# The attention's low halves of two batches: a VectorE subtraction becomes a TensorE pass and a ScalarE copy, in a new order

## The chip, the cores and the metric

The kernel runs on one core of one Trainium2 chip. The metric is device microseconds of one execution, from launch to end; a comparison takes the median of several. PE is TensorE, PEld its weight loads, DVE is VectorE, ACT is ScalarE, POOL is GpSimd, and SP is SyncE, which issues all the DMAs of this kernel.

## The reference

Three stages follow one another, all in float32: attention over pooled keys and values, a gated MLP with a convolution of three taps along the sequence, and a second gated MLP that mixes along the sequence.

```python
# q, k, v: (8, 8, 576, 64); keys and values are means over 8 neighbours
k_p = k.reshape(B, H, 72, 8, D).mean(axis=3)
v_p = v.reshape(B, H, 72, 8, D).mean(axis=3)
attn = softmax(q @ k_p.T / 8)             # 1e-9 added to the sum
x = (attn @ v_p).transpose(0, 2, 1, 3).reshape(8, 576, 512)
...
h = np.maximum(x @ w_in, 0.0)             # 512 -> 1024
conv_out = sum(conv_w[k] * shift(h, k - 1) for k in range(3))
x = h * sigmoid(conv_out) @ w_out
...
h = gelu(x @ w_in2)                       # 512 -> 1024, halves u and v
v_s = einsum('ts,bsd->btd', w_sg, normalize(v) * g_ln) + b_sg
out = x + (u * v_s) @ w_out2
```

## The kernel before

**Split numbers.** TensorE multiplies operands of the type fp32r. So that the result comes out as accurate as float32, an operand is held as two such numbers, a high half (the value rounded to fp32r) and a low half (the value less the high half, rounded again), and a product is a sum of three passes: high by high, low by high, high by low. Each operand therefore costs a rounding copy, mostly on ACT, and a subtraction, on DVE or POOL.

**Stages.** Batches are worked on one after another, 576 rows each. For a batch `t_k` and `t_v` pool keys and values, `t_kfin` and `t_vfin` lay them out as `KBT` and as `Vh`, `Vl`, `VR`; `t_qtr` transposes the queries (batches 0 and 1 by PE, the others by DVE); `t_s` forms the scores and the softmax; `t_e` transposes its result into `eTh` and `eTl`, again by PE for batches 0 and 1 (`B_DMA = 2`) and by way of DRAM and DVE (`xb`) for the others. `t_a` then multiplies by the values: for each pair of heads p and each half of the rows it sums four passes of 128 x 288 into a bank of PSUM and leaves the result, divided by 8 (the keys' and values' pool), as the high half `xT[0]` (tile `xh`) and the low half `xT[1]` (tile `xl`). The in-projection `t_i` reads `xh` and `xl`, 384 columns at a time and twelve passes for each of eight column blocks, and does the convolution and the gate on ACT and DVE; `t_o` is the out-projection. The second MLP follows from about 540 us on.

**What t_a does in batches 0 to 7.** Four passes on PE (L523, through the helper at L106), a copy of the bank times 1/8 by ACT into `xh` (L531), and one DVE instruction (L533) that takes the bank times 1/8 less `xh` into `xl`. The bank comes from `a_bank`, which has three buffers that scores, transposes and `t_a` share; it is free again when the DVE instruction has read it.

**Weights.** The weights arrive as 64-bit numbers. `to_f32` turns each 128 x 512 block into float32 with three DVE instructions (L146, L149, L152); ACT then copies the high half (L209) and POOL subtracts (L134). These 16 blocks (`wi0` to `wi7`, `w0` to `w7`) are needed in the first 120 us.

**Order.** Every engine runs its instructions in the order in which they are written, and that order is given by hand in the string `ORDER`: some 3,600 words such as `a2.0` (one more step of task `a`, part 2, batch 0), each of which runs one step of a generator up to its next `yield`. A waiting instruction holds up all that stands behind it on its engine. SP issues the DMAs in the same order.

Of the kernel before, what the change touches and what calls it, by code (L numbers as in the profile page):

```python
# [26 lines left out]
def pooled_attention_gated_mlps(  # L27
# [37 lines left out]
    TT = [(t * 128, min(128, S - t * 128)) for t in range((S + 127) // 128)]  # L65
    NM = S // 128
# [22 lines left out]
    def a_bank():  # L89
        return psum1.tile([128, 512], F32, tag="a", bufs=3, name="psa")  # L90
# [24 lines left out]
    ident = const.tile([128, 128], F32, name="ident")
    small = const.tile([128, 6], F32, name="small")
    mask, mhalf = small[0:96, 0:4], small[:, 4:6]
    coef = const.tile([128, 32], F32, name="coef")

    in1_ctx = ExitStack()  # L120
    in1 = in1_ctx.enter_context(tc.tile_pool(name="in1", bufs=1))
    att_ctx = ExitStack()
    att1 = att_ctx.enter_context(tc.tile_pool(name="att1", bufs=1, side="right"))
    att2 = att_ctx.enter_context(tc.tile_pool(name="att2", bufs=2, side="right"))
    KBT = att1.tile([128, NP_, 2 * SP], F32, name="KBT")
    Vh = att1.tile([128, NP_, 128], F32R, name="Vh")
    Vl = att1.tile([128, NP_, 128], F32R, name="Vl")
    VR = att1.tile([96, NP_, 128], F32R, name="VR")
    eTh = att1.tile([128, NP_ + 2, S], F32R, name="eTh")
    eTl = att1.tile([128, NP_, S], F32R, name="eTl")  # L130
# [5 lines left out]
    def to_f32(raw, t, tmp=None):  # L136

        w = raw.rearrange("p (n t) -> p t n", t=2)
        lo, up = w[:, 0, :], w[:, 1, :]
        ti = t.bitcast(U32)
        mi = ti if tmp is None else tmp.bitcast(U32)
        nc.vector.tensor_scalar(out=mi, in0=up, scalar1=3, scalar2=0x3FFFFFF8,  # L146
                                op0=ALU.logical_shift_left, op1=ALU.bitwise_and)
        yield
        nc.vector.scalar_tensor_tensor(out=mi, in0=up, scalar=0xC0000000, in1=mi,  # L149
                                       op0=ALU.bitwise_and, op1=ALU.bitwise_or)  # L150
        yield
        nc.vector.scalar_tensor_tensor(out=ti, in0=lo, scalar=29, in1=mi,  # L152
                                       op0=ALU.logical_shift_right, op1=ALU.bitwise_or)
        yield
# [22 lines left out]
    def t_coef(*_):  # L177
        n = 3 * NF
        cf = work.tile([128, 512], F32, tag="y", name="cf")
        raw = att2.tile([128, 1024], U32, tag="raw", name="craw")  # L180
        nc.sync.dma_start(out=raw[0:n, 0:256], in_=conv_w.rearrange("k (m p) -> (k m) p", p=256))
        nc.sync.dma_start(out=cf[n:n + NU, 0:128], in_=g_ln.rearrange("(m p) -> m p", p=128))
        yield
        yield from to_f32(raw[0:n, 0:256], cf[0:n, 0:128])
        ps = a_bank()
        n += NU
        nc.tensor.transpose(ps[:, 0:n], cf[0:n, 0:128], ident[0:n, 0:n])
        yield
        nc.scalar.copy(out=coef[:, 0:n], in_=ps[:, 0:n])

    def cw(kk, m):
        return coef[:, kk * NF + m:kk * NF + m + 1]

    def gl(m):
        return coef[:, 3 * NF + m:3 * NF + m + 1]


    def weight(pool_, tag, src, eng, bank_, done):
        raw = pool_.tile([128, 1024], U32, tag=tag, name=f"{tag}raw")
        dst = raw  # L200
        if len(src.shape) == 3:
            dst = raw.rearrange("p (a b) -> p a b", a=src.shape[1])
        nc.sync.dma_start(out=dst, in_=src)
        yield
        t = work.tile([128, 512], F32, tag="y", name="t")
        yield from to_f32(raw, t, bank_() if bank_ else None)
        hl = pool_.tile([128, 2, 512], F32R, tag=tag, name=f"{tag}hl")
        done(hl)
        nc.scalar.copy(out=hl[:, 0, :], in_=t)  # L209
        yield  # L210
        subtract(hl[:, 1, :], t, hl[:, 0, :], eng)
# [25 lines left out]
    def staged(name, n, where=None):  # L237

        if where is not None:
            p_, tag, size = where  # L240
            early[name] = [p_.tile([128, size], F32, tag=tag, name=name), 0]
        z, at = early[name]
        early[name][1] += 512 * n
        return z[:, at:at + 512 * n].rearrange("p (a s) -> p a s", a=n)
# [125 lines left out]
    qbs = {}  # L370
    qTs = {}

    def t_q(_, b):
        qb = att1.tile([128, len(TT) * DM], F32, tag="qb", name="qb")[:, 0:NP_ * S].rearrange("p (a s) -> p a s", a=NP_)
        for c in range(4):
            for pr in range(NP_):
                nc.sync.dma_start(
                    out=qb[32 * c:32 * c + 32, pr, :],
                    in_=q[b, 2 * pr + c // 2, :, 32 * (c % 2):32 * (c % 2) + 32].rearrange("(g i) d -> i g d", i=32),
                )  # L380
        qbs[b] = qb

    def t_qtr(t, b):
        t0, n = TT[t]
        if b < 2:
            if t == 0:
                if b == 0:
                    z = staged("q0", 5, (in1, "xl", XW * KC))
                else:
                    z = att1.tile([128, len(TT) * DM], F32, tag="qb", name="qb").rearrange("p (t d) -> p t d", d=DM)  # L390
                qbs[b] = z
            nc.sync.dma_start(out=qbs[b][0:n, t, :].rearrange("p (h d) -> p h d", h=H),
                              in_=q[b, :, t0:t0 + n, :].rearrange("h s d -> s h d"))
            yield
            ps = a_bank()
            for p in range(NP_):
                nc.tensor.transpose(ps[:, 128 * p:128 * p + n], qbs[b][0:n, t, 128 * p:128 * p + 128],
                                    ident[0:n, 0:n])
            yield
            qT = att2.tile([128, NP_, 128], F32, tag="qT", name="qT")  # L400
            nc.scalar.copy(out=qT[:, :, 0:n], in_=ps.rearrange("p (a s) -> p a s", a=NP_)[:, :, 0:n])  # L401
        else:
            qT = att2.tile([128, NP_, 128], F32, tag="qT", name="qT")
            nc.vector.transpose(out=qT[:, :, 0:n], in_=qbs[b][:, :, t0:t0 + n])
        qTs[b, t] = qT
# [104 lines left out]
    xT = {}  # L510
# [7 lines left out]
    def t_a(p, b):  # L518
        x0 = (b % 2) * (S + 2) + 1
        for hf in range(2):  # L520
            ps = a_bank()[:, 0:HS]
            T = slice(HS * hf, HS * hf + HS)
            mm_sum(ps, [  # L523
                (Vh[:, p, :], eTh[:, p, T]),
                (Vh[:, p, :], eTl[:, p, T]),
                (Vl[:, p, :], eTh[:, p, T]),
                (VR[:, p, :], eTh[0:96, NP_ + p // 2, T]),
            ])
            yield
            X = slice(x0 + HS * hf, x0 + HS * hf + HS)  # L530
            nc.scalar.activation(out=xT[0][:, p, X], in_=ps, func=AF.Copy, scale=1.0 / POOL)  # L531
            yield
            nc.vector.scalar_tensor_tensor(  # L533
                out=xT[1][:, p, X], in0=ps, scalar=1.0 / POOL, in1=xT[0][:, p, X].bitcast(F32),
                op0=ALU.mult, op1=ALU.subtract)
            yield
# [73 lines left out]
    w2 = {}  # L610
# [153 lines left out]
    def passes(ps, pairs, first, last):  # L764
        n = len(pairs)
        for i, (a, b_) in enumerate(pairs):
            nc.tensor.matmul(out=ps, lhsT=a, rhs=b_, start=first and i == 0, stop=last and i == n - 1,  # L767
                             skip_group_check=True)
# [191 lines left out]
    g2 = {}  # L960
# [126 lines left out]

    for key in ORDER.split():
        step(key)
# [30 lines left out]
```

## Time and profile before

| | before |
|---|---|
| time, median of 3 runs | 953.7 us (951.04, 953.7, 954.91) |
| the profiled execution, its own time | 952.67 us |
| its span, first to last instruction | 950.9 us |
| PE busy | 918.5 us (97%) |
| PE weight loads busy | 838.4 us (88%) |
| DVE busy | 759.8 us (80%) |
| ACT busy | 527.6 us (55%) |
| POOL busy | 553.5 us (58%) |
| mean granted TensorE clock | 0.993 of 2.4 GHz |

The span leaves out 1.77 us of the execution's own time. An engine's busy time is the time in which at least one of its instructions runs; PE's matmuls overlap, so that one takes longer from start to end than the next needs to start after it. In the profile an idle time is put down to the instruction that the engine waited for, its releaser.

### The profile page before, as it was taken

How to read it: one execution, taken by the hardware profiler on the slowest of the kernel's cores; microseconds unless marked ns; L12 is line 12 of the kernel's file. 1: busy time of each engine (PE TensorE's matmuls, PEld its weight loads, DVE VectorE, ACT ScalarE, POOL GpSimd, SP SyncE). 2: the span in 40 equal slices, each digit the busy share in tenths (PEclk: the TensorE clock that was granted, in tenths of full speed). 3: DMA queues.
4: the chain of work that ended last, by engine and by line, in shares of the span. 5: the costliest groups of instructions: out<-in, count | busy, mean ns of one | idle time of the engine just before them, and what ended most of it. 6: DMA issues, size and time to landing. Idle time of an engine off the chain costs nothing.

```text
span 950.9 us, 15815 instructions
## 1 busy us (share of the span) xinstructions
PE 918.5 (97%) x5396; PEld 838.4 (88%) x5396; DVE 759.8 (80%) x1399; ACT 527.6 (55%) x1108; POOL 553.5 (58%) x630
## 2 busy tenths in 40 slices
PE   5899999999999999999999999999999899999998
PEld 4787789988899899998998899999999898999886
DVE  5889988879879687787687878888787977878574
ACT  3666576766667576666655757655656432323211
POOL 3696788785868676557245375643553665555331
PEclk9899999999999999999999999999999999999999
DMA  9986293744635644424380475466537755565734
GB/s 230 251 197 149 62 186 114 178 133 139 153 119 139 142 119 100 129 59 117 99 170 34 94 144 141 151 184 200 146 111 230 246 176 190 158 192 173 231 115 142
DMA packets 185900, 143.61 MB, mean 151 GB/s; under 512 B 106048, under 2 KB 140124, under 8 KB 185820
## 3 DMA queue, kind: packets, MB, share of 16 engines
q1 hardware_dynamic: 185820, 142.61, 56.4%
q8 instruction: 42, 0.69, 0.3%
q14 instruction: 38, 0.31, 0.1%
HBM read 94.20 MB, written 48.37 MB: 150 GB/s over the span
## 4 chain that ended last, share of the span: by engine, by line
PE 77%; DVE 9%; DMA 6%; POOL 2%; ACT 2%; issue 2%; SPq 1%; DVEq 0%; POOLq 0%; ACTq 0%
PE psi L106 19%; PE pso L767 12%; PE psa L767 12%; PE pso L99 6%; PE pso L101 6%; PE pso L100 6%; PE psi L101 3%; PE psi L99 3%; PE psi L100 3%; PE psa L106 3%; PE psa L419 3%; DMA st<-in_v_dram 2%; DMA res<-x2s 1%; DMA wi1raw<-in_moe_w_in_dram 1%; DVE psi L571 1%
## 5 line engine op out<-in xcount | busy, mean ns | idle before, releaser
L134 POOL TENSOR_TENSOR hg<-g,hg 128x384 fp32r<-128x384 f32 x96 | 97.5, 1023 | 64.0 <-ACT hg L580 60.3
L1001 POOL TENSOR_TENSOR u<-u,tmp 128x288 f32<-128x288 f32 x64 | 61.8, 986 | 56.0 <-DVE tmp L997 39.8
L573 ACT ACTIVATE psi<-psi 128x384 f32<-128x384 f32 x96 | 46.1, 480 | 68.2 <-DVE psi L571 68.1
L570 DVE SCALAR_TENSOR_TENSOR psi<-h,coef,psi 128x384 f32<-128x384 f32 x96 | 58.9, 614 | 26.4 <-ACT psi L568 25.4
L134 POOL TENSOR_TENSOR eTl<-xb,eTh 128x512 fp32r<-128x512 f32 (+1 forms) x30 | 45.3, 1510 | 50.2 <-ACT eTh L503 50.1
L708 POOL TENSOR_TENSOR xb<-xb 128x768 f32<-128x768 f32 x24 | 45.9, 1912 | 48.2 <-DVE xc L134 30.2
L558 ACT ACTIVATE h<-psi 128x386 f32<-128x386 f32 (+1 forms) x96 | 47.3, 493 | 43.6 <-PE psi L106 43.3
L577 DVE SCALAR_TENSOR_TENSOR g<-psi,h 128x384 f32<-128x384 f32 x96 | 52.4, 546 | 20.0 <-ACT psi L573 18.1
L617 ACT CAST sc<-vf 128x512 fp32r<-128x512 f32 x48 | 28.8, 618 | 63.1 <-POOL vf L948 27.8
L571 DVE SCALAR_TENSOR_TENSOR psi<-h,coef,psi 128x384 f32<-128x384 f32 x96 | 59.8, 623 | 3.4
L419 PE MATMUL psa<-KBT,qT 128*128 128x144 f32 (+1 forms) x320 | 54.0, 299 | 5.2 <-ACT qT L401 1.8
L568 ACT ACTIVATE psi<-h,coef 128x384 f32<-128x384 f32 x96 | 56.2, 586 | 3.1
L419 PEld LDWEIGHTS psa<-KBT,qT 128*128 128x128 f32 (+1 forms) x320 | 45.2, 184 | 12.8 <-ACT qT L401 2.4
L580 ACT CAST hg<-g 128x384 fp32r<-128x384 f32 x96 | 47.7, 507 | 10.1 <-DVE g L577 10.0
L767 PE MATMUL pso<-wc,xc 128*128 128x256 f32 x378 | 51.1, 283 | 1.3 <-ACT tmp L790 0.9
L767 PE MATMUL psa<-wc,xc 128*128 128x256 f32 x378 | 50.7, 282 | 0.8 <-ACT tmp L790 0.5
L767 PEld LDWEIGHTS pso<-wc,xc 128*128 128x128 f32 x378 | 48.5, 189 | 2.5 <-ACT tmp L790 1.3
L1016 ACT CAST g<-u 128x256 fp32r<-128x256 f32 x64 | 22.3, 402 | 50.4 <-POOL u L1001 43.2
L767 PEld LDWEIGHTS psa<-wc,xc 128*128 128x128 f32 x378 | 48.6, 189 | 1.4 <-ACT tmp L790 0.7
L767 PE MATMUL psa<-xc,wc 128*128 128x384 f32 x252 | 48.2, 338 | 0.3 <-ACT tmp L834 0.3
L767 PE MATMUL pso<-xc,wc 128*128 128x384 f32 x252 | 48.3, 338 | 0.0
L457 POOL TENSOR_TENSOR en<-e,rs 128x512 f32<-128x512 f32 (+1 forms) x30 | 32.7, 1091 | 23.2 <-ACT h L558 8.5
(397 smaller groups left out, 3106.0 us busy)
## 6 DMA issues: line engine op xcount, KB each, us to landing
xb<-eds SPq DMA_DIRECT2D x24, 384.0 KB, 3.1
x2s<-ob SPq DMA_DIRECT2D x36, 256.0 KB, 2.8
us<-ub SPq DMA_DIRECT2D x24, 384.0 KB, 3.3
vs<-vg SPq DMA_DIRECT2D x18, 512.0 KB, 3.7
u<-us SPq DMA_DIRECT2D x16, 576.0 KB, 5.0
vf<-vs SPq DMA_DIRECT2D x16, 512.0 KB, 3.8
out_dram<-ob SPq DMA_DIRECT2D x32, 256.0 KB, 2.9
xb<-x2s SPq DMA_DIRECT2D x40, 192.0 KB, 4.3
```

Source lines behind the costliest of these rows:

```text
L99: nc.tensor.matmul(out=out_, lhsT=ah, rhs=bh, start=first, stop=False)
L100: nc.tensor.matmul(out=out_, lhsT=al, rhs=bh, start=False, stop=False)
L101: nc.tensor.matmul(out=out_, lhsT=ah, rhs=bl, start=False, stop=last)
L106: nc.tensor.matmul(out=out_, lhsT=a, rhs=b_, start=(i == 0), stop=(i == n - 1))
L134: eng.tensor_tensor(out=out, in0=in0, in1=hi.bitcast(F32), op=ALU.subtract)
L419: nc.tensor.matmul(out=ps[0:n, 2 * SP * x:2 * SP * x + 2 * SP], lhsT=qT[:, p, 0:n], rhs=KBT[:, p, :], start=True, stop=True)
L568: nc.scalar.activation(out=y, in_=tap(1), func=AF.Copy, scale=cw(1, f))
L570: nc.vector.scalar_tensor_tensor(out=y, in0=tap(0), scalar=cw(0, f), in1=y, op0=ALU.mult, op1=ALU.add)
L571: nc.vector.scalar_tensor_tensor(out=y, in0=tap(2), scalar=cw(2, f), in1=y, op0=ALU.mult, op1=ALU.add)
L577: nc.vector.scalar_tensor_tensor(out=go, in0=y, scalar=1.0, in1=tap(1), op0=ALU.add, op1=ALU.mult)
L767: nc.tensor.matmul(out=ps, lhsT=a, rhs=b_, start=first and i == 0, stop=last and i == n - 1, skip_group_check=True)
L1001: pool.tensor_tensor(out=z, in0=z, in1=o, op=ALU.mult)
```

## The change

In `t_a`, for batches 0 and 1 alone, the DVE instruction goes. In its place PE adds to the same bank a fifth pass, the high half `xh` times a new constant `minus` (minus 8 times the identity, 128 x 128), and ACT copies what is then in the bank, times 1/8, to `xl`. The five passes go through `passes`, which starts the bank's sum at the first pass and ends it at the fifth; the ACT copy to `xh` reads the sum in between. `minus` is made once by an ACT instruction in `t_coef`. Batches 2 to 7 are as before.

The tile `qb` holds 2,304 numbers for each partition in place of 2,560: of batch 1's five pieces of queries the last, of 64 rows, now lies in the tile `xb` (named `qe` there). `ORDER` is written anew from end to end; it has 16 words more, two for each of `a0.0` to `a3.1`.

```diff
-ORDER = '''z k0.0 k1.0 k2.0 z z p0.0 c p1.0 p2.0 v0.0 v1.0 p3.0 p4.0 v2.0 i0 i1 z z k0.1 p0.0 k1.0 ...'''
+ORDER = '''z k0.0 k1.0 k2.0 z z p0.0 c p1.0 p2.0 v0.0 v1.0 p3.0 p4.0 v2.0 i0 i1 z z k0.1 v2.1 p0.1 ...'''
...
+    minus = const.tile([128, 128], F32R, name="minus")
...
         nc.scalar.copy(out=coef[:, 0:n], in_=ps[:, 0:n])
+        nc.scalar.activation(out=minus, in_=ident, func=AF.Copy, scale=-float(POOL))
...
-                    z = att1.tile([128, len(TT) * DM], F32, tag="qb", name="qb").rearrange("p (t d) -> p t d", d=DM)
-                qbs[b] = z
+                    z = att1.tile([128, NM * DM], F32, tag="qb", name="qb").rearrange("p (t d) -> p t d", d=DM)
+                qbs[b] = [z[:, i, :] for i in range(NM + 1 - b)]
+            if b and t == NM:
+                qbs[b].append(att1.tile([128, 4 * EQ], F32, tag="xb", name="qe")[:, 0:DM])
...
-            mm_sum(ps, [
+            passes(ps, [
                 (Vh[:, p, :], eTh[:, p, T]),
                 (Vh[:, p, :], eTl[:, p, T]),
                 (Vl[:, p, :], eTh[:, p, T]),
                 (VR[:, p, :], eTh[0:96, NP_ + p // 2, T]),
-            ])
+            ], True, b >= B_DMA)
             yield
             X = slice(x0 + HS * hf, x0 + HS * hf + HS)
             nc.scalar.activation(out=xT[0][:, p, X], in_=ps, func=AF.Copy, scale=1.0 / POOL)
             yield
-            nc.vector.scalar_tensor_tensor(
-                out=xT[1][:, p, X], in0=ps, scalar=1.0 / POOL, in1=xT[0][:, p, X].bitcast(F32),
-                op0=ALU.mult, op1=ALU.subtract)
+            if b < B_DMA:
+                passes(ps, [(minus, xT[0][:, p, X])], False, True)
+                yield
+                nc.scalar.activation(out=xT[1][:, p, X], in_=ps, func=AF.Copy, scale=1.0 / POOL)
+            else:
+                nc.vector.scalar_tensor_tensor(
+                    out=xT[1][:, p, X], in0=ps, scalar=1.0 / POOL, in1=xT[0][:, p, X].bitcast(F32),
+                    op0=ALU.mult, op1=ALU.subtract)
             yield
```

Three places of the order follow; a row is a line of the kernel, an operation, and the tile that it writes with those that it reads, with buffer numbers. The names are those of the section on the kernel; `st1` is batch 1's raw keys, `ident` the identity.

First PE at the end of batch 0's `t_a`, ahead of the first in-projection (`psi`, `wi0hl`). Before:

```order
L106 MATMUL psa_625<-eTh_135,VR_134 128x288
L106 MATMUL psa_636<-eTh_135,Vh_132 128x288
L106 MATMUL psa_636<-eTl_136,Vh_132 128x288
L106 MATMUL psa_636<-eTh_135,Vl_133 128x288
L106 MATMUL psa_636<-eTh_135,VR_134 128x288
L106 MATMUL psa_652<-ident_119,st1_174 64x128 x16
L106 MATMUL psi_687<-xh_475,wi0hl_465 128x386
```

And now:

```order
L776 MATMUL psa_629<-eTh_136,VR_135 128x288
L776 MATMUL psa_618<-xh_440,minus_122 128x288
L776 MATMUL psa_638<-eTh_136,Vh_133 128x288
L776 MATMUL psa_638<-eTl_137,Vh_133 128x288
L776 MATMUL psa_638<-eTh_136,Vl_134 128x288
L776 MATMUL psa_638<-eTh_136,VR_135 128x288
L776 MATMUL psa_629<-xh_440,minus_122 128x288
L106 MATMUL psa_661<-ident_119,st1_175 64x128 x8
L776 MATMUL psa_638<-xh_440,minus_122 128x288
L106 MATMUL psa_661<-ident_119,st1_175 64x128 x8
L401 MATMUL psa_707<-ident_119,qb_178 128x128 x4
L106 MATMUL psi_712<-xh_440,wi0hl_480 128x386
```

A bank's fifth pass stands one set of four passes behind its own set, the last one eight key matmuls behind. ACT in the same place, before:

```order
L531 ACTIVATE xh_475<-psa_599 128x288
L531 ACTIVATE xh_475<-psa_605 128x288
L531 ACTIVATE xh_475<-psa_625 128x288
L352 CAST Vh_132<-vp_554 32x4x64 x4
L531 ACTIVATE xh_475<-psa_636 128x288
L209 CAST wi4hl_650<-t_610 128x512
```

And now:

```order
L535 ACTIVATE xh_440<-psa_606 128x288
L535 ACTIVATE xh_440<-psa_618 128x288
L540 ACTIVATE xl_413<-psa_606 128x288
L535 ACTIVATE xh_440<-psa_629 128x288
L540 ACTIVATE xl_413<-psa_618 128x288
L540 ACTIVATE xl_413<-psa_629 128x288
L535 ACTIVATE xh_440<-psa_638 128x288
L211 CAST wi4hl_658<-t_611 128x512
L540 ACTIVATE xl_413<-psa_638 128x288
L211 CAST wi6hl_674<-t_555 128x512
```

The four copies to `xh` are now woven with four to `xl`, and batch 1's `Vh` comes after them. The second place is PE in the middle of batch 1's `t_a`. Before:

```order
L488 MATMUL psa_1321<-ident_119,en_1236 32x64 x2
L106 MATMUL psa_1328<-eTh_135,Vh_132 128x288
L106 MATMUL psa_1328<-eTl_136,Vh_132 128x288
L106 MATMUL psa_1328<-eTh_135,Vl_133 128x288
L106 MATMUL psa_1328<-eTh_135,VR_134 128x288
L419 MATMUL psa_1338<-KBT_131,qT_1305 128x144 x2
```

And now:

```order
L492 MATMUL psa_1321<-ident_119,en_1302 32x64 x2
L776 MATMUL psa_1334<-eTh_136,Vh_133 128x288
L776 MATMUL psa_1334<-eTl_137,Vh_133 128x288
L776 MATMUL psa_1334<-eTh_136,Vl_134 128x288
L776 MATMUL psa_1334<-eTh_136,VR_135 128x288
L776 MATMUL psa_1334<-xh_440,minus_122 128x288
L423 MATMUL psa_1342<-KBT_132,qT_1265 128x144 x2
```

Here the fifth pass stands right behind its own four, with ACT's copy to `xh` between them. The third place is SP, the loads of the first 50 us. Before:

```order
L268 DMA raw_369<-in_k_dram 128x2x512
L203 DMA wi3raw_380<-in_moe_w_in_dram 128x4x256
L233 DMA st1_174<-in_v_dram 32x2x512 x4
L203 DMA wi4raw_441<-in_moe_w_in_dram 128x4x256
L203 DMA wi6raw_449<-in_moe_w_in_dram 128x4x256
L268 DMA st1_174<-in_k_dram 128x2x512
L392 DMA qb_183<-in_q_dram 128x8x64
L203 DMA wi5raw_595<-in_moe_w_in_dram 128x4x256
L203 DMA wi7raw_622<-in_moe_w_in_dram 128x4x256
```

And now:

```order
L205 DMA wi3raw_319<-in_moe_w_in_dram 128x4x256
L235 DMA st1_175<-in_v_dram 32x2x512 x4
L205 DMA wi6raw_365<-in_moe_w_in_dram 128x4x256
L205 DMA wi4raw_380<-in_moe_w_in_dram 128x4x256
L270 DMA raw_456<-in_k_dram 128x2x512
L205 DMA wi5raw_504<-in_moe_w_in_dram 128x4x256
L396 DMA qb_178<-in_q_dram 128x8x64
L205 DMA wi7raw_644<-in_moe_w_in_dram 128x4x256
L205 DMA w0raw_648<-in_moe_w_out_dram 128x1024
L396 DMA qe_652<-in_q_dram 64x8x64
L270 DMA st1_175<-in_k_dram 128x2x512
```

Batch 1's values (`st1` from `in_v`) come ahead of one load of batch 2's keys (`raw`), and the second load of batch 1's keys (`st1` from `in_k`) comes behind `wi5`, `wi7`, `w0` and two loads of queries.

## Rows read from the trace of the kernel before

**Rows 1.** The page, part 1: busy us, share of the span, instructions.

```profile
PE 918.5 (97%) x5396; PEld 838.4 (88%) x5396; DVE 759.8 (80%) x1399; ACT 527.6 (55%) x1108; POOL 553.5 (58%) x630
```

**Rows 2.** Windows: length, busy us (instructions) of each engine, granted clock, DMA share, GB/s.

```profile
0.00:44.00 44.00, 30.14 (x196) 24.42 (x196) 30.20 (x61) 21.30 (x55) 21.98 (x47) 0.92 1.07 234
44.00:120.00 76.00, 71.32 (x448) 62.39 (x447) 70.53 (x140) 48.20 (x110) 55.84 (x78) 1.00 0.60 143
120.00:540.00 420.00, 416.99 (x2208) 376.42 (x2208) 340.66 (x620) 279.20 (x559) 271.76 (x327) 1.00 0.50 123
540.00:740.00 200.00, 197.65 (x1351) 192.60 (x1351) 163.05 (x287) 121.49 (x249) 103.86 (x87) 1.00 0.59 164
740.00:951.00 211.00, 202.44 (x1200) 182.54 (x1199) 155.36 (x293) 57.39 (x138) 100.03 (x93) 0.99 0.57 180
```

**Rows 3.** PE's waits from 60 to 145 us: us in total, times, longest.

```profile
PE psi L106 <- DVE g L577: 1.6, 3, 0.6
...
PE psa L419 <- DVE xl L533: 0.6, 1, 0.6
```

**Rows 4.** PE's timeline in batch 0's t_a: start, duration, shapes.

```profile
47.23 0.29 PE L106 MATMUL psa<-eTh,Vl 128*128 128x288 f32 x1
47.36 0.30 PE L106 MATMUL psa<-eTh,VR 96*128 96x288 f32 x1
47.61 0.40 PE L106 MATMUL psa<-eTh,Vh 128*128 128x288 f32 x1
47.85 0.30 PE L106 MATMUL psa<-eTl,Vh 128*128 128x288 f32 x1
```

**Rows 5.** One bank's way through PE, ACT and DVE (timelines of each).

```profile
38.85 0.29 PE L106 MATMUL psa<-eTh,VR 96*128 96x288 f32 x1
...
39.19 0.41 ACT L531 ACTIVATE xh<-psa 128x288 fp32r<-128x288 f32 x1 [0.46 <-PE psa L106]
...
39.80 0.46 DVE L533 SCALAR_TENSOR_TENSOR xl<-psa,xh 128x288 fp32r<-128x288 f32 x1
```

**Rows 6.** Groups by form, all batches: busy us, mean ns of one, idle before.

```profile
L533 DVE SCALAR_TENSOR_TENSOR xl<-psa,xh 128x288 fp32r<-128x288 f32 x64 | 27.6, 445 | 4.4 <-ACT xh L531 3.9
...
L531 ACT ACTIVATE xh<-psa 128x288 fp32r<-128x288 f32 x64 | 25.5, 409 | 14.2 <-PE psa L106 12.9 <-issue 0.8
L346 ACT COPY vp<-psa 128x128 f32<-128x128 f32 x4 | 1.0, 260 | 1.6 <-PE psa L106 1.6
```

**Rows 7.** The instructions of L533 that start between 44 and 120 us: min/median/max ns.

```profile
L533 DVE SCALAR_TENSOR_TENSOR xl<-psa,xh x10: 406/450/460, 47.1 to 115.8; 128x288 fp32r<-128x288 f32 x10
```

**Rows 8.** Loads of the first 60 us: sum, landing times of tile st, SP, PE.

```profile
DMA packets 17502, 14.18 MB, mean 236 GB/s; under 512 B 10008, under 2 KB 14132, under 8 KB 17497
...
DMA to landing us min/median/max: 4.5/8.5/11.3
...
46.17 1.54 SPq L203 DMA_DIRECT2D w0raw<-in_moe_w_out_dram  x1
...
41.55 2.02 PE L106 MATMUL psa<-st,ident 128*128 128x128 f32 x16 [0.61 <-DMA st<-in_v_dram]
...
54.30 4.78 PE L106 MATMUL psa<-ident,st 128*64 128x128 f32 x48
```

**Rows 9.** Tile eTh on DVE (min/median/max ns); two waits of PE; a window.

```profile
L134 DVE TENSOR_TENSOR eTh<-xb,eTh x30: 284/704/4131, 133.2 to 461.0; 32x256 fp32r<-32x256 f32 x24, 32x128 fp32r<-32x128 f32 x6
...
211.86 0.40 PE L106 MATMUL psa<-eTh,VR 96*128 96x288 f32 x1 [1.24 <-DVE eTh L134]
...
231.04 0.40 PE L106 MATMUL psa<-eTl,Vh 128*128 128x288 f32 x1 [0.73 <-POOL eTl L134]
...
232.00:233.00 1.00, 1.00 (x6) 1.00 (x5) 0.97 (x2) 0.52 (x2) 0.00 (x0) 0.50 0.29 92
```

**Rows 10.** PE's waits over the whole span: two later ones.

```profile
PE pso L767 <- DVE tmp L997: 2.4, 3, 1.1
...
PE pso L767 <- DVE sc L134: 1.1, 1, 1.1
```

More of the change, by code (lines that the diff above doesn't have):

```diff
@@ L373, in t_q @@
     def t_q(_, b):
-        qb = att1.tile([128, len(TT) * DM], F32, tag="qb", name="qb")[:, 0:NP_ * S].rearrange("p (a s) -> p a s", a=NP_)
+        qb = att1.tile([128, NP_ * S], F32, tag="qb", name="qb").rearrange("p (a s) -> p a s", a=NP_)
         for c in range(4):
@@ L389, in t_qtr @@
                 else:
-                    z = att1.tile([128, len(TT) * DM], F32, tag="qb", name="qb").rearrange("p (t d) -> p t d", d=DM)
-                qbs[b] = z
-            nc.sync.dma_start(out=qbs[b][0:n, t, :].rearrange("p (h d) -> p h d", h=H),
+                    z = att1.tile([128, NM * DM], F32, tag="qb", name="qb").rearrange("p (t d) -> p t d", d=DM)
+                qbs[b] = [z[:, i, :] for i in range(NM + 1 - b)]
+            if b and t == NM:
+                qbs[b].append(att1.tile([128, 4 * EQ], F32, tag="xb", name="qe")[:, 0:DM])
+            nc.sync.dma_start(out=qbs[b][t][0:n, :].rearrange("p (h d) -> p h d", h=H),
                               in_=q[b, :, t0:t0 + n, :].rearrange("h s d -> s h d"))
@@ L396, in t_qtr @@
             for p in range(NP_):
-                nc.tensor.transpose(ps[:, 128 * p:128 * p + n], qbs[b][0:n, t, 128 * p:128 * p + 128],
+                nc.tensor.transpose(ps[:, 128 * p:128 * p + n], qbs[b][t][0:n, 128 * p:128 * p + 128],
                                     ident[0:n, 0:n])
```

2 lines of the change are left out of this document (1 added, 1 removed).

## The prediction

> **What bounds the kernel now.** I read the page first: PE is busy for 918.5 us, 97% of the span, DVE for 80% [rows 1]. So the span is PE's work plus PE's idle time, and a change is worth what it does to those two. The windows by stretch say where the 32.4 us of idle time lie [rows 2]: 13.9 before 44 us, where the loads run without a break, 4.7 from 44 to 120 us, 3.0 from 120 to 540, 2.3 from 540 to 740, and 8.6 behind that. In the second stretch DVE is busy for 70.5 of 76 us, 93%, more than in any other, and the list of PE's waits from 60 us on names DVE in all its seven rows, 4.5 us together, the gate's g first; only one, 0.6 us, is for the low half xl itself [rows 3]. So this stretch is where DVE holds PE up, and the most that a lighter DVE can return in it is 4.7 us.
>
> **The change part by part**, against the profiled execution's own 952.67 us, 1.0 below the median of 953.7.
>
> *What goes from DVE.* 16 instructions of 0.445 us [rows 6], 7.1 us; ten of them, 4.4 us busy, start in the tight stretch [rows 7], four before it and two after. The stretch's DVE share falls from 93% to 87%. From 120 to 540 us DVE is 81% busy and PE idles 0.7% of the time, against 6.2% here [rows 2]; a straight line between the two gives 3.5% at 87%, which is 2.6 us of idle time and a gain of 2.1. The four instructions before 44 us let the weights' conversion start ahead of time, so I take a little more, -3.0; the ends are 0 (the waits are chains of latency, not a full queue) and -4.7.
>
> *What PE gets.* 16 passes of 288 columns. Behind a pass of its own kind one starts 0.13 us after the last; behind a change of work or a wait it takes 0.24 [rows 4]. 16 of them cost 2.1 to 3.8 us; most stand among other passes of this size, so 0.15, +2.4. None of it is hidden, since PE sets the end; only what falls before 41.5 us, where PE waits 0.6 us for batch 1's values anyway [rows 8], is partly absorbed: -0.5 (0 to -1.0).
>
> *The new wait.* A fifth pass waits for ACT's copy to xh, and PE's whole queue stands behind it. From a set's last pass to the end of that copy is 39.60 less 39.14, 0.46 us, and some 0.05 for the hand-over [rows 5], so 0.5 us must be covered by other PE work. In the order two of the 16 stand right behind their own set (the first of batch 0 and the one shown in batch 1) and a third has one single pass between: 1.4 us less what they overlap with the waits of the first 41 us. Five have one set of four passes between, 0.52 us, which just covers it if ACT comes at once; the other eight have more than a microsecond of work between them. Sum +1.4; ends 0.4 and 4.0 (eight of them late by 0.5).
>
> *What ACT gets.* 16 copies of 0.409 us and one of `minus`, 0.26 us [rows 6]. In the tight stretch ACT is busy for 48.2 of 76 us; ten more copies make 52.3, 69%, beside 66% from 120 to 540 us, where PE hardly waits [rows 2]. I cost it at nothing beyond the new wait; the cover is ACT's idle third. The Trainium skill (ScalarE: Activation LUTs, "Rules for kernel authors") speaks against this half of the change: multiplications and additions belong on VectorE, which it puts at up to three times the speed in bf16. By that rule ACT would pay more than DVE saves; here, from PSUM and in these types, the rows have 0.409 against 0.445 us, so the sum stays.
>
> *What the order moves on SP.* Batch 1's values come 0.5 MB sooner, 2 us at 236 GB/s, and the wait of 0.6 us at 41.55 goes [rows 8]. The second load of batch 1's keys now stands about where `w0` stood, behind some 7 MB of loads; `w0` was issued at 46.17 us, and such a load lands 4.5 to 11.3 us after issue, 8.5 in the middle: at about 54.7, where it landed far ahead before. PE first needs it behind the first in-projection block, where the last key matmuls, 24 in the order and 48 records in the trace, started at 54.30 us [rows 8]. So -0.6 and +0.6 (0 to +2.5): nothing.
>
> *All else in the order.* Behind 125 us the work is the same and is only ordered anew: 0, with -3 and +4 as what the waits listed there could lose or gain (below).
>
> Sum: -3.0 + 2.4 - 0.5 + 1.4 = **+0.3**: 953.0 us on the profiled execution's scale, **954.0** on the median's.
>
> **The rivals.** (1) *Faster: the new order also takes out late waits.* PE waits 2.4 us for tmp and 1.1 for sc near the end [rows 10] and 1.2 for eTh at 211.86, and runs from 232 to 235 us at 1.2 GHz (granted clock 0.50; the first of three such windows is shown) after a wait of 0.73, 1.5 us of work lost [rows 9]. Half of these 6.2 us, with the rest of the tight stretch (-1.7) and new waits at their low end (-1.0), gives 948.2. For it: all these waits end at DVE, or at POOL behind it. Against it: DVE's load after 125 us is unchanged, and only its order is new.
>
> (2) *Slower: a long DVE subtraction lands in front of PE.* The subtraction eTh<-xb takes 0.70 us in the middle and up to 4.13; the removed L533 takes 0.41 to 0.46 wherever it stands in the tight stretch [rows 7, 9]. So some DVE work is stretched by what runs beside it, and the order decides by what. One that is longer by 3.4 us and not covered by PE's queue, with 1.5 us at 1.2 GHz behind it and one more wait of 1.2 us, makes +6.1: 960.1. It decides from the point at which the subtraction is stretched by more than the PE work that stands between it and its first reader, as in the wait of 1.24 at 211.86 [rows 9].
> The Trainium skill (SBUF — State Buffer, "Who interferes with whom") has a rule for it: a VectorE instruction with two SBUF operands waits while a GpSimd instruction that reads SBUF holds the port they share, and one with a single SBUF operand does not. The trace agrees on both kinds: eTh<-xb has two, L533 one. By that rule the removed instructions free POOL of nothing, which leaves the sum as it is.
>
> (3) *The key load is late.* If it lands after 55 us PE idles until it does: up to +2.5, 956.5. (4) *ACT becomes the bound of t_a.* A bank is now held through two copies and a pass of PE, three banks go round, and ACT serves casts between: the new wait at its upper end, +2.6: 956.6. (5) *The change doesn't do what it says:* PE's waits are chains through ACT and DVE that a lighter DVE leaves as long as they are; the gain is 0, +3.0: 957.0.
>
> **How the numbers follow.** This kernel's measurement can tell some 0.5%, 4.8 us, from no change: below 948.9 counts as faster, above 958.5 as slower. Forecast 0.48, rival 1 0.15, rival 2 0.11, rival 3 0.10, rivals 4 and 5 0.08 each. Forecast and rivals 3, 4 and 5 lie within the band; two of the last three together would leave it, 0.01. So faster 0.15, same 0.73, slower 0.12. The range runs from rival 1's time, 948.2, whose lower half I leave out, to 958.8, where rivals 3 to 5 are in and most of rival 2 is out.
>
> **What would show it.** The windows by stretch: from 44 to 120 us of before's work DVE's share near 87% and PE's idle time near 2 us plus the new waits. Fifth passes 0.13 to 0.24 us apart from their forerunner; a wait of about 0.5 us for xh at the two places shown, and little elsewhere. The wait for batch 1's values gone; one for its keys of at most a microsecond. Behind 125 us PE's idle time within a few microseconds of 13.9. The prediction is wrong if PE idles as much in the tight stretch although DVE is lighter, if waits for xh add up to more than 3 us, or if the stretches after 125 us differ by more than 4 us.

## The result and the profile after

The changed kernel takes **942.2 us** (median of 4, 941.8 to 944.0) beside 954.2 for the kernel before (median of 4): 0.988 of its time, 95% interval 0.986 to 0.991, about 11 us less. Measured again later, beside 25 runs of before: 943.0 us, 0.990 (0.987 to 0.992). Forecast was 954.0, with 948.2 as the lower end. The forecast was wrong, in size and in kind: the time fell by more than 1%. Three executions among all that follow, one each of before, e_alone and new_early_dve, took 2,286 to 4,902 us; no time below counts them.

The page, part 1, of the changed kernel (busy us, share, instructions), as in [rows 1]:

```profile
PE 915.5 (97%) x5412; PEld 839.1 (89%) x5412; DVE 757.6 (81%) x1383; ACT 534.6 (57%) x1125; POOL 558.0 (59%) x630
```

PE has 16 instructions more, DVE 16 fewer, as announced. The windows, with the columns of [rows 2]:

```profile
0.00:44.00 44.00, 29.98 (x190) 24.57 (x191) 29.78 (x59) 22.34 (x56) 21.36 (x46) 0.88 1.08 237
44.00:120.00 76.00, 73.98 (x473) 65.44 (x472) 66.91 (x130) 54.16 (x128) 57.51 (x82) 1.00 0.55 146
120.00:540.00 420.00, 419.67 (x2236) 379.65 (x2235) 341.44 (x624) 281.56 (x560) 279.14 (x329) 1.00 0.49 124
540.00:740.00 200.00, 196.46 (x1364) 192.85 (x1363) 166.67 (x294) 123.18 (x251) 106.44 (x88) 1.00 0.60 174
740.00:940.00 200.00, 195.43 (x1157) 176.59 (x1155) 152.81 (x280) 53.36 (x132) 93.58 (x89) 0.99 0.55 175
```

Length less PE's busy time is PE's idle time. From 44 to 120 us it is 2.0 us (4.7 before), with DVE busy for 88% (93% before): what the prediction wanted to see there. Behind 120 us it is 0.3, 3.5 and 4.8, 8.6 together, where before had 13.9: that was to stay as it was.

These idle times add up to 24.7 us against 32.4, a difference of 7.7, while the span fell by 10.7. The page understates what PE loses: a pass of 288 columns is on record for 0.29 us and the next can start 0.13 us later [rows 4], so a gap of up to 0.16 us leaves no idle time at all, and a stretch at 1.2 GHz is fully busy [rows 9]. The Trainium skill (Perfetto Trace Analysis, "Identifying the Most-Contended Engine") says that matmuls' busy share is no good measure of how close a kernel is to its roofline, since they are pipelined. These two traces agree that busy time misses loss, by the 3 us between 7.7 and 10.7.

So I worked out a second measure from the trace: for each matmul but the last, the time from its start to the next one's, less the lower quartile of that for matmuls of its form in both traces. What is left is time lost between the first matmul (at 8.5 and 8.9 us) and the last, and the sum of the quartiles is PE's work: 879.3 us before, 881.4 after (2.1 more for the 16 passes, 0.13 each). Lost, by stretches of before's time and the same work in the changed kernel:

| stretch of before, us | lost before, us | lost after, us |
|---|---|---|
| 0 to 44 | 15.1 | 15.4 |
| 44 to 125 | 12.0 | 8.1 |
| 125 to 198 | 2.7 | 2.6 |
| 198 to 250 | 7.1 | 0.8 |
| 250 to 590 | 6.9 | 7.6 |
| 590 to 700 | 4.3 | 4.1 |
| 700 to the end | 9.9 | 6.2 |
| all | 58.0 | 44.8 |

Three stretches differ: 3.9 us from 44 to 125 us, less the 2.1 for the passes; 6.3 from 198 to 250; 3.7 at the end. The low halves of two batches are done by 125 us. The largest piece lies behind them, in 52 us. The windows of that piece, first before:

```profile
198.00:250.00 52.00, 49.10 (x256) 43.42 (x255) 43.99 (x75) 32.47 (x69) 38.30 (x50) 0.97 0.49 125
225.00:236.00 11.00, 9.34 (x38) 7.37 (x37) 10.31 (x22) 7.90 (x20) 5.14 (x8) 0.84 0.46 135
```

and after:

```profile
198.00:250.00 52.00, 51.98 (x287) 47.73 (x287) 44.90 (x86) 36.78 (x73) 41.16 (x54) 1.00 0.59 148
225.00:236.00 11.00, 11.00 (x68) 10.50 (x67) 9.03 (x19) 8.92 (x24) 9.13 (x13) 1.00 0.53 128
```

PE starts 287 matmuls where it started 256, never idles, and the granted clock stays at 1.00; before had 0.84 in the narrow window, 3.4 us of it at 1.2 GHz.

**What held PE up there, in the trace of before.** DVE's timeline (start, duration, idle time before and its releaser):

```profile
205.54 0.69 DVE L404 STREAM_TRANSPOSE qT<-qb 128x512 f32<-128x512 f32 x1
209.78 0.38 DVE L298 COPY KBT<-psa 64x216 f32<-64x216 f32 x1 [3.54 <-ACT KBT L296]
...
210.32 1.48 DVE L134 TENSOR_TENSOR eTh<-xb,eTh 32x256 fp32r<-32x256 f32 x1
...
219.65 4.13 DVE L134 TENSOR_TENSOR eTh<-xb,eTh 32x256 fp32r<-32x256 f32 x1
```

ACT's, with what DVE waited for:

```profile
208.14 0.49 ACT L558 ACTIVATE h<-psi 128x386 f32<-128x386 f32 x1 [1.34 <-PE psi L106]
208.67 0.59 ACT L568 ACTIVATE psi<-h,coef 128x384 f32<-128x384 f32 x1
209.19 0.39 ACT L295 COPY KBT<-psa 64x288 f32<-64x288 f32 x1
```

DVE stands still for 3.54 us because ACT's copy to batch 4's `KBT` is queued behind a copy to `h`, and that waits for PE's twelve passes. So DVE's subtraction `eTh<-xb` comes late, and PE waits for it at 211.86 [rows 9]. Nine microseconds later the same kind of subtraction takes 4.13 us, while POOL works without a break beside it:

```profile
219.67 0.45 POOL L253 TENSOR_TENSOR raw<-raw 64x128 f32<-64x128 f32 x1
220.09 1.97 POOL L134 TENSOR_TENSOR hg<-g,hg 128x384 fp32r<-128x384 f32 x2
222.02 1.28 POOL L251 TENSOR_TENSOR raw<-raw 128x512 f32<-128x512 f32 x1
```

POOL's last row ends at 223.30 us and the subtraction at 223.78, 0.48 us later; "Rival 2" below takes this up. Behind it DVE is late for the next gate and the next low half, PE waits four times between 226 and 231 us, the last time for 0.73 [rows 9], and then runs at 1.2 GHz for 3.4 us, from about 232 to 235.

The waits come with the old order in every execution, the slow clock behind them in some only. Ten of the 18 profiles have the old order here, and all ten show the waits of 1.2 and 0.7 us. Four of them have 3.4 us at 1.2 GHz between 229 and 245 us, and six stay at 2.4 GHz, as the other eight profiles do. One of the six is new_late (below), whose waits from 198 to 250 us and clock are:

```profile
PE psa L106 <- DVE eTh L134: 1.2, 1, 1.2
...
PE psa L106 <- POOL eTl L134: 0.7, 1, 0.7
...
225.00:236.00 11.00, 9.39 (x50) 7.50 (x50) 10.32 (x22) 7.88 (x20) 5.24 (x9) 1.00 0.50 137
```

So some 1.7 of the 6.3 us in the table, half of 3.4, is a loss that the old order has in some executions only.

### The profile page after: what moved, and what is told of

It is laid out like the page before. It is cut to its first block, busy times and chain, and to the rows that moved or that the text cites. A ratio compares the mean times of both kernels' runs of the same rounds, so it can differ in the third digit from the quotient of the medians.

```text
span 940.2 us, 15870 instructions
## 1 busy us (share of the span) xinstructions
PE 915.5 (97%) x5412; PEld 839.1 (89%) x5412; DVE 757.6 (81%) x1383; ACT 534.6 (57%) x1125; POOL 558.0 (59%) x630
## 4 chain that ended last, share of the span: by engine, by line
PE 86%; DVE 7%; ACT 2%; DMA 2%; issue 1%; SPq 0%; POOL 0%; DVEq 0%; ACTq 0%; POOLq 0%
PE psi L106 21%; PE psa L776 17%; PE pso L776 13%; PE pso L99 7%; PE pso L101 7%; PE pso L100 7%; PE psa L423 4%; PE psi L101 3%; PE psi L99 3%; PE psi L100 3%; PE psa L106 1%; DMA vf<-vs 1%; DVE sc L135 1%; DVE mx L434 1%; DMA q<-in_q_dram 1%
## 5 line engine op out<-in xcount | busy, mean ns | idle before, releaser
L135 POOL TENSOR_TENSOR hg<-g,hg 128x384 fp32r<-128x384 f32 x96 | 99.9, 1049 | 70.7 <-ACT hg L589 69.8
L135 DVE TENSOR_TENSOR sc<-vf,sc 128x512 fp32r<-128x512 f32 x48 | 41.2, 869 | 8.0 <-ACT sc L626 8.0
```

The costliest lines, as they stand in the source:

```text
L135: eng.tensor_tensor(out=out, in0=in0, in1=hi.bitcast(F32), op=ALU.subtract)
```

## The experiments

Theory 1, from the table: the new order itself takes out the waits behind 125 us; the low halves matter ahead of that only. Theory 2: the lighter DVE of the first 125 us lets all its later work come sooner. Each run is compared with runs of the kernel before on the same chip. Words of `ORDER` stand in the diffs: those of order_alone, new_early and new_early_dve are against the changed kernel, that of halves_spread is against halves_alone, the others are against the kernel before.

### Order and low halves, each alone

**order_alone**: the new order, DVE's subtraction kept.

```diff
-            ], True, b >= B_DMA)
+            ], True, True)
...
-            if b < B_DMA:
-                passes(ps, [(minus, xT[0][:, p, X])], False, True)
-                yield
...
-e3.0 a0.0 a1.0 a3.0 e3.0 a0.0 i5 a3.0 a0.0 a0.0 a3.0
+e3.0 a0.0 a1.0 a3.0 e3.0 a0.0 i5 a3.0 a0.0
```

> The new order without the low halves on TensorE: the words for the 16 fifth passes are left out and DVE subtracts where ACT's second copy stood. Theory 1 (the new order itself takes out waits behind 125 us, about 6 us from 198 to 250 us and some 3 behind 590 us; the low halves matter in the first 125 us alone): 945 us, 943 to 947. Theory 2 (the gain behind 125 us is the lighter DVE's, which lets all its later work come sooner): 952 to 955, as before.

Measured: 946.9 us, 0.994 (0.992 to 0.997), 5 us faster. That is inside the range of Theory 1 and outside that of Theory 2: the order gains without a lighter DVE. But 2 us more were expected.

**halves_alone**: the change in `t_a`, the old order with two words more for each task.

```diff
-k1.3 k1.3 t6 a0.1 O5.0 I1.1 a2.1 p4.2
+k1.3 k1.3 t6 a0.1 a3.1 O5.0 I1.1 a3.1 a2.1 p4.2
```

> The low halves on TensorE in the old order: each fifth pass stands behind the first four passes of other work that follow its own set, ACT's second copy where DVE subtracted or two words later. Theory 1: only the first 125 us change, DVE's relief of up to 3.3 us less 2.1 for the passes: 953 us, 951.5 to 955. Theory 2: 944 to 946, as the changed kernel.

Measured: 960.2 us, 1.009 (1.007 to 1.011), 8 us slower. Neither theory had that. PE's waits from 41 to 128 us have a new first line (us in total, times, longest), and its longest is this one, in the timelines of PE and then of ACT:

```profile
PE psa L776 <- ACT xh L535: 4.3, 4, 2.5
```

```profile
119.33 0.40 PE L776 MATMUL psa<-xh,minus 128*128 128x288 f32 x1 [2.46 <-ACT xh L535]
```

```profile
118.34 0.62 ACT L211 CAST w6hl<-t 128x512 fp32r<-128x512 f32 x1 [0.84 <-DVE t L153]
118.87 0.40 ACT L535 ACTIVATE xh<-psa 128x288 fp32r<-128x288 f32 x1
```

The fifth pass waits for ACT's copy, that one is queued behind a cast of weights, and the cast waits for DVE. Here the price of the pass is not its 0.13 us but what stands ahead of ACT's copy. (The smaller `qb` and the piece `qe` come with this kernel too; no wait of PE names `qe`.)

**halves_spread**: the same, with each pass where PE, by the trace of before, comes after that copy.

```diff
-k1.3 k1.3 t6 a0.1 a3.1 O5.0 I1.1 a3.1 a2.1 p4.2
+k1.3 k1.3 t6 a0.1 O5.0 I1.1 a3.1 a3.1 a2.1 p4.2
```

> The low halves on TensorE in the old order, with each fifth pass put where PE, by the trace of before, comes after ACT's copy to xh has ended, as far as the three banks and the first reader let it. Theory A (halves_alone lost 8 us because the passes stood where ACT's copy, queued behind other work, came late; the form itself costs little): 953 to 956 us. Theory B (in the old order the form costs as much wherever the passes stand, because banks are held longer): 959 to 961.

Measured: 960.1 us, 1.009 (1.006 to 1.011). Theory A falls. The waits for `xh` are down to 0.5 us, and others have come (PE's waits, 30 to 125 us):

```profile
PE psa L776 <- ACT xl L540: 3.1, 3, 2.2
PE psa L106 <- ACT xl L540: 2.9, 2, 2.7
...
PE psa L776 <- ACT xh L535: 0.5, 1, 0.5
```

These PE instructions start new work in one of the three banks (`psa`) and wait until ACT's second copy has left it. A pass that comes later holds its bank longer: put early it waits for ACT's first copy, put late others wait for ACT's second. That was rival 4, and in the old order, with either of the two placements that were run, the kernel is 8 us slower.

### Where the order's gain lies

**new_mid**: the old order, from its word 546 (about 125 us) to word 1240 (292 us) the new one. At the first joint:

```diff
-I1.1 I3.1 I3.1 V.2 s2.2 e0.2 v0.3 I3.1 s2.2 q.3
+I1.1 v1.3 O1.0 s2.2 I3.1 q.3 e0.2 I3.1 I2.1 s4.2
```

> The kernel before, with the new order only between about 125 and 292 us of its time; the order ahead of it and behind it is the old one, as far as steps are not already done. Theory 1: the waits of 1.4 us at 211.9, of 0.4 to 1.0 from 226 to 230, and the stretch at 1.2 GHz behind them go, 6 us: 948 us, 947 to 949.5. Rival (those waits depend on how early DVE comes to 125 us): 952 or more.

Measured: 946.1 us, 0.994 (0.992 to 0.996), 5.8 us faster. Theory 1 holds, its rival falls: what precedes 125 us is as before.

**new_late**: the old order up to word 2425 (598 us), the new one behind it.

```diff
-O1.8 n0.1 n2.0 u1.1 u1.1 u1.1 T5.2 n0.1 n0.1 T7.2
+O0.11 T5.2 u1.1 u1.1 u1.1 u1.1 u1.1 n0.1 n0.1 n2.0
```

> The kernel before, with the new order only behind about 598 us. Theory 1: the excess steps of PE at 610, from 745 to 760 and at 898 us are the order's: 951 us, 949.5 to 952. Rival (they depend on what POOL and DVE have left undone earlier): 953.5 to 955.

Measured: 949.5 us, 0.998 (0.996 to 0.999), 2.4 us faster, as Theory 1 had it, and the wait for `sc` of [rows 10] is gone from PE's list.

**new_early** and **after_again**: the changed kernel with the old order behind its word 560 (122 us), and the changed kernel once more.

```diff
-s2.2 I3.1 t7 q.3 e0.2 I3.1 I2.1 s4.2 I4.1 I3.1
+a2.0 t7 I4.1 I3.1 I3.1 V.2 s2.2 e0.2 v0.3 I3.1
```

> The changed kernel with its order and its low halves on TensorE up to about 122 us, and behind that the old order. Theory 1 (5.8 us from 198 to 250 us and 2.4 behind 598 us are the order's there, as the two spliced kernels have shown; what is left of the gain, about 3 us, is made in the first 125 us): 949 us, 947 to 951. Theory 2 (the lighter DVE of the first 125 us brings the gain behind it as well, which the old order would then keep): 942 to 945.

> The changed kernel once more, as a yardstick beside the other three runs of this call: 941 us, 940 to 943, if the median of the first comparison holds; nothing is told apart by it.

Measured: 949.9 us, 0.998 (0.996 to 1.000), 2.2 us faster; and 943.0, 9.1 us faster. Theory 2 falls a second time. The three parts, 2.2, 5.8 and 2.4, make 10.4 us, between the 9.1 and the 11 to 12 of the two measurements of the whole.

**new_early_dve**: as new_early, with DVE's subtraction.

```diff
-                passes(ps, [(minus, xT[0][:, p, X])], False, True)
...
+            nc.vector.scalar_tensor_tensor(
...
-s2.2 I3.1 t7 q.3 e0.2 I3.1 I2.1 s4.2 I4.1 I3.1
+a2.0 t7 I4.1 I3.1 I3.1 V.2 e0.2 v0.3 I3.1 s2.2
```

> The new order up to about 125 us with DVE's subtractions, the old order behind it: as new_early, which came out 2 us faster than before, without the low halves on TensorE. From order_alone (5 us faster, of which 8 are made behind 125 us), estimated: 3 us slower than before, 955 us, 953.5 to 956.5; then the low halves are worth 5 us in the new order. Rival (the early part of the new order is good for either form, and order_alone lost elsewhere): 950 to 952.

Measured: 955.2 us, 1.004 (1.002 to 1.005), 4 us slower than before. So in the early part the two edits need each other: the old order with low halves on PE loses 8 us, the new one without them 4, both together gain 2. That is why order_alone fell short. PE's waits from 36 to 125 us of this kernel:

```profile
PE psi L106 <- DVE g L581: 1.4, 2, 1.2
PE psa L771 <- DVE xl L537: 1.4, 2, 1.2
PE psa L106 <- DVE eTh L135: 1.3, 1, 1.3
PE psa L423 <- DVE eTh L135: 1.2, 1, 1.2
PE psa L492 <- DVE xl L537: 0.6, 1, 0.6
```

These and the shorter ones that name DVE make 7.3 us, where new_early has 1.9.

### Two words

**local_before, k_alone, e_alone**: the kernel before with one step `K.4` moved ahead of `I4.3`, with one step `e3.3` moved behind nine words (five DVE instructions), and each of the two alone.

```diff
-p0.4 I4.3 e2.3 K.4 K.4 s4.3
+p0.4 K.4 I4.3 e2.3 K.4 s4.3
...
-a3.3 e3.3 I7.3 I6.3 I6.3 O2.0 k2.5 I3.3 I4.3 s0.4 I6.3 s0.4
+a3.3 I7.3 I6.3 I6.3 O2.0 k2.5 I3.3 I4.3 s0.4 I6.3 e3.3 s0.4
```

> The kernel before with two words of its order moved: ACT's copies to batch 4's KBT ahead of the copy to h that waited for PE (DVE waited 3.5 us for them at 206 us), and DVE's subtraction eTh<-xb of batch 3, which took 4.13 us at 219.65, behind eight steps, so that six DVE instructions go ahead of it. Theory 1 (these two hold DVE up, DVE holds up PE at 211.9 and from 226 to 230, and TensorE's clock falls behind that): 947 us, 946 to 949. Rival (the stretch is stretched as long by whatever stands there, or the wait comes at another place): 951 to 953.

> The kernel before with the first of the two moves alone: ACT's copies to batch 4's KBT ahead of the copy to h. Theory A (DVE's idle time of 3.5 us at 206 us is behind the wait of 1.2 us at 211.9 alone): 1.4 us less, 950.7 us, 950 to 951.5. Theory B (the idle time sets DVE back for all that follows, the long subtraction and the waits from 226 to 230 too): 947, as both moves together.

> The kernel before with the second move alone: six DVE instructions go ahead of the subtraction eTh<-xb that took 4.13 us. Theory A (the subtraction, stretched by what POOL does beside it, makes the waits from 226 to 230 us and the stretch at 1.2 GHz): 3.9 us less, 948 us, 947 to 949.5. Theory B (it comes from the idle time at 206 us): 951 to 952.

Measured: both 946.9 us, 0.994 (0.992 to 0.997), 5.2 us faster, nearly as much as the whole new order between 125 and 292 us. The first alone 949.3, 0.997 (0.996 to 0.999), 2.5 us; the second alone 949.5, 0.998 (0.996 to 1.000), 2.2 by the medians and 1.8 by the ratio. Theory A holds for both in kind, and 2.5 and 2.2 add up to about the 5.2: each word has its own wait. In size the first word gained more than the 1.4 us that Theory A gave it, and the second less than 3.9; the clock, different from one execution to the next, is not told apart here. DVE's rows, and the last of POOL's beside the subtraction, with both moves:

```profile
206.42 0.38 DVE L298 COPY KBT<-psa 64x216 f32<-64x216 f32 x1 [1.00 <-ACT KBT L296]
...
219.73 1.62 DVE L134 TENSOR_TENSOR eTh<-xb,eTh 32x256 fp32r<-32x256 f32 x1
...
219.56 1.31 POOL L251 TENSOR_TENSOR raw<-raw 128x512 f32<-128x512 f32 x1
```

with the first alone:

```profile
206.69 0.38 DVE L298 COPY KBT<-psa 64x216 f32<-64x216 f32 x1 [1.00 <-ACT KBT L296]
...
217.51 4.09 DVE L134 TENSOR_TENSOR eTh<-xb,eTh 32x256 fp32r<-32x256 f32 x1
...
219.83 1.29 POOL L251 TENSOR_TENSOR raw<-raw 128x512 f32<-128x512 f32 x1
```

and with the second alone:

```profile
209.38 0.38 DVE L298 COPY KBT<-psa 64x216 f32<-64x216 f32 x1 [3.54 <-ACT KBT L296]
...
221.82 1.51 DVE L134 TENSOR_TENSOR eTh<-xb,eTh 32x256 fp32r<-32x256 f32 x1
...
221.57 1.28 POOL L251 TENSOR_TENSOR raw<-raw 128x512 f32<-128x512 f32 x1
```

The subtraction takes 4.1 us where it stood, whatever DVE did before, and 1.5 to 1.6 five instructions later. In all three, as in before, it ends 0.47 or 0.48 us after this instruction of POOL. The first word shortens DVE's idle time from 3.54 to 1.00 us, and PE's wait for `eTh` goes; the second takes out PE's waits of 0.7, 0.4 and 0.2 us behind the long subtraction and leaves one of 0.7 for the gate (0.3 before).

**local_and_late**: local_before, and the new order behind 598 us, with the joint of new_late.

```diff
-p0.4 I4.3 e2.3 K.4 K.4 s4.3
+p0.4 K.4 I4.3 e2.3 K.4 s4.3
...
-O1.8 n0.1 n2.0 u1.1 u1.1 u1.1 T5.2 n0.1 n0.1 T7.2
+O0.11 T5.2 u1.1 u1.1 u1.1 u1.1 u1.1 n0.1 n0.1 n2.0
```

> The kernel before with the two moved words and the new order behind about 598 us, without the low halves on TensorE. If the parts add up (5.2 and 2.4 us): 944.3 us, 943 to 946, and all but some 2 us of the whole gain is had without them. Rival (the late part depends on what stands ahead of it): 946.5 to 949.

Measured: 945.4 us, 0.993 (0.991 to 0.995), 5.9 us faster by the medians and 6.5 by the ratio; 7.6 was the sum of its parts, which lies inside the interval (4.4 to 8.5). Without the low halves on TensorE more than half of the gain is had; the changed kernel stays the fastest that was run.

### The relief of DVE by itself

**no_xl, no_xl_late_fill, no_xl_clean**: the kernel before without the 16 subtractions; `xl` filled with zeros by POOL at once, or in two parts later, or not at all, with `xh` read in its place. All three leave the low halves out of batches 0 and 1, and the last counts a product with `xh` twice.

```diff
-            nc.vector.scalar_tensor_tensor(
...
+            if b >= B_DMA:
+                nc.vector.scalar_tensor_tensor(
...
-            prs += [(w_[:, 0, kt, :], xT[0][:, kt, X]), (w_[:, 0, kt, :], xT[1][:, kt, X]),
+            prs += [(w_[:, 0, kt, :], xT[0][:, kt, X]), (w_[:, 0, kt, :], xT[c >= 3][:, kt, X]),
```

In the first two the last pair of lines is not changed, and POOL fills instead:

```diff
+            for kc in range(KC):
+                nc.gpsimd.memset(z[:, kc, 1:S + 1], 0.0)
...
+    def t_fill(i, *_):
+        for kc in range(KC):
+            nc.gpsimd.memset(xT[1].bitcast(F32)[:, kc, (S + 2) * i + 1:(S + 2) * i + S + 1], 0.0)
```

> The kernel before without the 16 DVE subtractions of batches 0 and 1 and with nothing in their place: the low halves of these batches are left out (POOL fills xl with zeros once, about 35 us after the start). It measures the relief of DVE by itself, in the old order. Prediction on record for this term: 3.0 us less, 0 to 4.7: 949 us, 947 to 952. Rival (the waits are chains that a lighter DVE leaves as long): 952.

> Again the kernel before without the 16 DVE subtractions, whose results are left out; POOL now fills xl with zeros behind xh's borders and, for batch 1, where it idled at 85 us, since in the first such kernel the filling stood in front of ACT's first copy to xh and cost 2.1 us of PE. Prediction on record for the relief: 3.0 us less, 0 to 4.7. From the steps of PE between 55 and 147 us in that kernel's trace, estimated: 2.0 less, 950 us, 948.5 to 951.5. Rival (a lighter DVE gives nothing): 952 or more.

> The kernel before without the 16 DVE subtractions of batches 0 and 1, and the in-projection of these batches reads xh where it read xl, so that nothing need be filled (the low halves of these batches are left out). The relief of DVE by itself in the old order. On record: 3.0 us less, 0 to 4.7, 949 us. Theory A (the waits for DVE between 41 and 125 us that fell in the first two kernels, 2 us, come back as time): 949.5 to 950.5. Theory B (other work is late next, the relief gives nothing): 951.5 to 952.5.

Measured: 953.9 us, 1.002 (1.000 to 1.003); 953.8, 1.001 (0.999 to 1.003); 951.6, 1.000 (0.998 to 1.001). The first two say little: their traces show PE waiting 2.1 us at 39.6 and 1.9 us for `w4hl` behind POOL's filling. The third has no filling, and no gain. PE's waits from 41 to 122 us:

```profile
PE psa L106 <- DMA st<-in_v_dram: 3.4, 1, 3.4
PE psi L106 <- DVE g L578: 1.2, 3, 0.6
PE psa L419 <- DVE KBT L298: 0.6, 1, 0.6
```

The waits for DVE fell to 3.0 us from 4.5 [rows 3], and by the starts of the same matmuls in both traces 1.8 us come back between 90 and 115 us; the time doesn't show it, within 2 us.

**double_xl**: each of the 16 subtractions twice.

```diff
-            nc.vector.scalar_tensor_tensor(
+            for _ in range(2 if b < B_DMA else 1):
+                nc.vector.scalar_tensor_tensor(
```

> The kernel before with each of these 16 subtractions done twice, 7.1 us more for DVE. Theory A (DVE's load in the stretch from 44 to 125 us turns into PE's idle time, as the prediction has it): 3 us more or above, 955 us, 954 to 958. Theory B (it lies beside other waits): 951.5 to 953.

Measured: 955.4 us, 1.004 (1.002 to 1.006), 3.6 us slower by the ratio. Load put on DVE there costs half of its 7.1 us; load taken off gives nothing that the time shows. A straight line through the present load is wrong on one side.

## Why the prediction was wrong, step by step

**The failed step: "Behind 125 us the work is the same and is only ordered anew: 0".** It measured 5.8 us up to 292 us and 2.4 behind 598; which words make the 2.4, no run shows. Its ground, that DVE's load there is unchanged, is true (341 us busy from 120 to 540 in both) and proves nothing: two words moved, at equal load, gave 5.2. The waits were all in the rows. The 1.24 at 211.86, the 0.73 at 231.04, the clock at 0.50 and the subtraction of 4.13 [rows 9] were all read; the first and the clock were priced, with two later waits [rows 10], at 6.2 us, and rival 1 then took half of it at a chance of 0.15. That mechanism was right. What was missing was one step further back in each chain: DVE's idle 3.54 us behind ACT, and POOL's unbroken run beside the long subtraction. Both are faults of an order, not of load; with them seen, an order written anew from end to end is likelier to lose them than to keep them.

**Rival 2 stood on the wrong side.** The stretched subtraction was in the kernel before, and the new order took it out (0.82 us at the same place). The Trainium skill (SBUF — State Buffer, "Who interferes with whom") gave the kind: two SBUF operands beside a POOL instruction that reads SBUF. The trace of before agrees. Of its 24 subtractions of 32x256, the seven that meet POOL at rest take 0.61 to 0.63 us; of the 17 that start beside a POOL instruction all but one end 0.46 to 0.50 us after a POOL instruction has ended. Mostly that is the first to end. At 210.32 it is the second (1.48 us in all), and at 219.65 the sixth, which makes the 4.13; why five were let by there, no run shows. So what counts is where in POOL's queue the subtraction meets it, not whether POOL is busy.

**DVE's relief, -3.0.** Mis-sized for the kernel before: -0.4 us, interval -2.1 to 1.3. The waits shrink, and 1.8 us come back in that trace, which lies inside the interval. That execution also waited 3.4 us at 41 for batch 1's values; some executions whose early part is that of before have this wait too (last section), and whether the relief has a share in it is not shown. In the new order the same 16 subtractions are worth 5.3 us, 955.2 less 949.9 (5.5 by the ratios, as the two ran on different chips), passes paid. The prediction asked what the relief does to the old waits; it had to ask which order goes with it.

**The passes, +2.4.** From each fifth pass's start to the next matmul's it is 4.1 us over all 16, 3.75 in the second profile: at the upper end of 2.1 to 3.8 and just above it. Four take 0.13, the others 0.22 and more. One of each kind, from PE's timeline:

```profile
42.48 0.40 PE L776 MATMUL psa<-xh,minus 128*128 128x288 f32 x1 [0.30 <-ACT xh L535]
...
48.88 0.29 PE L776 MATMUL psa<-eTh,VR 96*128 96x288 f32 x1
49.01 0.29 PE L776 MATMUL psa<-xh,minus 128*128 128x288 f32 x1
```

**The new wait, +1.4**: 1.1 us, 0.3 in the second profile. PE's waits in the first from 36 to 122 us:

```profile
PE psa L776 <- ACT xh L535: 1.1, 3, 0.5
PE psa L423 <- DVE e L436: 0.6, 2, 0.4
PE psa L776 <- DVE g L586: 0.5, 1, 0.5
```

Right in size or below it, and the waits for the gate are down from 1.6 to 0.5 us, as announced. But "ACT at nothing" holds for this order alone: in the old one rival 4 came true, and the same passes cost 5 to 7 us of waits for ACT.

**SP, 0**: the wait for batch 1's values is gone in both profiles. The wait for its keys that was priced at 0.6 us is missing in the first and there in the second (PE's waits, 36 to 122 us):

```profile
PE psa L106 <- DMA st<-in_k_dram: 0.6, 1, 0.6
```

The 0.6 for the values was one value of a wait that differs from execution to execution (last section). The fall of the early part as a whole, -2.2 measured, lies between the forecast's +0.3 and its lower bounds.

## What to carry to other kernels

Where an in-order queue bounds a kernel, its engine's load tells little about its waits: follow each wait on the bound engine two releasers back, to an idle time or an overlong instruction, and ask whether an edit of the order moves that very pair. If so, the order is a term of the sum with its own price, not a margin around zero. An edit that lengthens the life of a shared bank, and the order that was fitted to it, are one change: tested apart they lost 8 and 4 us, together they gained 2.

## What the hardware showed beside that

One and the same early part ran differently from execution to execution. In the profile of new_mid, whose first 125 us are the instructions of before, PE waits at 41 us (PE's waits, 36 to 44 us)

```profile
PE psa L106 <- DMA st<-in_v_dram: 3.0, 1, 3.0
```

where before has 0.6 and local_before nothing, and the window behind it is at half the clock:

```profile
41.00:48.00 7.00, 5.15 (x25) 4.76 (x26) 1.77 (x4) 1.47 (x7) 1.59 (x4) 0.52 1.12 301
```

which is 1.00 in before. That execution took 949.3 us, 3 more than the median of its kernel. Of the seven profiles whose first 125 us are the instructions of before, four have no such wait, the others 0.6, 2.8 and 3.0 us. Between 20 and 60 us PE ran at 1.2 GHz for 0 to 13.7 us in the 18 profiles. (The windows give no slow clock for the first 13 us, though PE's passes of 144 columns follow one another by 0.24 us there in before, and by 0.12 behind 13.3 us.) A difference of 3 us between two single traces ahead of 45 us says nothing here; medians of many runs do.

And PE reads as busy in time that it loses: by starts, 58.0 us were lost in the kernel before between its first matmul and its last, of which the page shows 19.2 as idle. The rest of the page's 32.4 lies ahead of the first (8.5) and behind the last (4.6).
